# Weight words of the gated block not held back, norms and gated products at other places of the order, one root on GpSimd

## The chip, the cores and the metric

The kernel runs on one core of a Trainium2 chip. Time is device time in microseconds (us) of one execution; the engines are TensorE (PE, the matrix products), VectorE (DVE), ScalarE (ACT), GpSimd (POOL) and SyncE (SP, whose queue issues the DMA transfers). Each engine runs its own instructions in order, and semaphores make one wait for another.

## The reference

Three steps on 4 batches of 576 rows. Attention with 8 heads of 64: a local part (a band of 3 rows to each side) plus a part that is computed on rows averaged by four and repeated. Its output x (576 x 512 per batch) goes through a mixing block and a gated block; all weights and inputs are fp32.

```python
# mixing block
X = np.fft.fft(x, axis=1); X = np.fft.fft(X, axis=2)
mixed = np.real(X)
u = x + mixed
un = (u - mean(u)) / np.sqrt(var(u) + 1e-06)
ch = np.maximum(un @ w_ch1, 0.0) @ w_ch2        # 512 -> 2048 -> 512
x = u + ch
# gated block
gate = 1 / (1 + np.exp(-conv5(x, conv_w)))       # causal, per column, 5 taps
out = (gate * (x @ w_val)) @ w_out
```

## The kernel before

The rows are worked on transposed, 512 columns on 4 x 128 partitions, in 12 units of 192 rows: unit n is rows 192j to 192j+191 of batch b, n = 3b + j, counted from 0. For a unit the kernel does, one after the other: the norm (`ln`), the products with w_ch1 (`mlp_steps`: ph, L1143) and w_ch2 (pc, L1163), and the gated block (`moe2_steps`): taps, products with w_val (val, L1255), and the out tiles with w_out (L1271). Products run as three passes of f16 halves: hh and hl are the high and low half of a hidden group, uh and ul of a normed unit, yy of x, gh and gl of the gated product. Attention of a batch (scores dS, exponentials dP, their transposes dPT and dO, then sc, eT and po of the averaged part) and its Fourier products (ab, pp, pn) are spread between the units of the batch before; batch 1's stand between units 0 to 2.

The norm of a unit (`ln`, L1004 to 1071) is a chain: sum over columns (two adds uc on POOL or DVE, then st on PE, L1020), subtract (uc), square (sq, ACT), the sum again (st), variance plus epsilon (vv), an inverse square root (`root`, L1046: an integer guess and two steps; seven operations with two fused on DVE, nine on GpSimd), the multiply of uc, and the halves uh (ACT) and ul (DVE). The first ph of the unit reads them.

The weights arrive as fp32 and are cut to their words by `to_f32` (L301): one TENSOR_SCALAR (L304) and two SCALAR_TENSOR_TENSOR (L166) on DVE for each raw tile of 128 x 512. For w_val and w_out (`word_w`, L329) there are eight raws. They go through two buffers, tags "k" and "v" of one pool; the next load into a buffer can be issued once the last raw in it has been read for the last time. Afterwards the scale is measured (cv on PE, L408) and the words are converted (L380 on ACT, L166 on DVE). `to_f32` takes a gate, an instruction behind which the words are issued; for w_val and w_out it is unit 3's multiply of uc, set in `ln`.

The order is written as positions: every step is put at a number, all are sorted by it (1.0 is the length of one unit's two products; n to n+1 is unit n), and a scheduler then fixes each engine's order by readiness and by priority offsets (`U`: norms 3000, taps, outs and words 0, values 1000). S_W3 is the stretch of numbers of the weight steps, P_T that of taps, values and outs of units 0 to 2, P_LN the place of a unit's norm behind the start of the unit before it, ROOT_G the norms whose root is on GpSimd. SP's queue is in order as well.

Of the kernel before, what the change touches and what calls it, by code (L numbers as in the profile page):

```python
# [12 lines left out]
I32 = mybir.dt.int32  # L13
# [8 lines left out]
UT = 192  # L22
# [34 lines left out]
S_C1 = (0.48, 0.5)  # L57
S_N0 = -7.5
S_W2 = (-7.4, -6.9)
S_W3 = (2.0, 2.28)  # L60
N_WARM = (8, 5, 14, 2, 2, 2)
S_G1 = (-6.8, -6.7)
S_G2 = (0.2, 0.44)
P_D = {1: (0.02, 1.2), 2: (2.31, 3.3), 3: (4.4, 6.0)}
P_E = {1: (1.21, 1.75), 2: (3.35, 4.4), 3: (6.1, 7.4)}
P_L = {1: 1.9, 2: 4.8, 3: 8.5}
P_T = {0: ((2.3, 2.5), (2.6, 2.8), (3.0, 3.01)), 1: ((2.8, 3.1), (3.15, 3.35), (3.4, 3.6)), 2: ((3.4, 3.6), (3.65, 3.85), (3.9, 4.2))}
EN_G = (1,)
SUM_V = ()
LN_PE = ((0, 0), (0, 1))  # L70
S_N1 = 0.1
S_N2 = 0.9
# [3 lines left out]
P_VAL = (0.38, 0.65)  # L76
P_OUT = (1.12, 1.75)
P_LN = 0.1
ROOT_G = ((0, 1),)
S_R0 = 0.8  # L80
D1_H = 0
LN_H = ()
# [46 lines left out]
def attn_moe_kernel(ctx, tc, q_t, k_t, v_t, w1, w2, w_val, conv_t, w_out, c_feat, c_seq, c_band, c_eye, out):  # L129
    nc = tc.nc  # L130
    P = 128
# [21 lines left out]
    V, A, G, T = nc.vector, nc.scalar, nc.gpsimd, nc.tensor  # L153
# [14 lines left out]
    def mul(eng, out, a, b):  # L168
        return eng.tensor_tensor(out=out, in0=a, in1=b, op=ALU.mult)
# [4 lines left out]
    def urgent(f, key):  # L174
        if U[key]:
            with tc.high_priority(offset=U[key]):
                f()
        else:
            f()
# [91 lines left out]
    W = [wp.tile([P, 1024], F32, name="W0")]  # L271
# [16 lines left out]
    def rows(dst, src, c, c0, n):  # L288
        load(out=dst, in_=src[c * 128:(c + 1) * 128, 2 * c0:2 * (c0 + n)])
# [3 lines left out]
    def behind(gate, f):  # L293

        if gate is None:
            f()
        else:
            with tc.issue_after(gate):
                f()

    def to_f32(dst, raw, gate=lambda: None):  # L301

        r = raw.rearrange("p (n t) -> p n t", t=2)
        behind(gate(), lambda: V.tensor_scalar(out=dst, in0=r[:, :, 1], scalar1=3, scalar2=0x3FFFFFF8,  # L304
                                               op0=ALU.logical_shift_left, op1=ALU.bitwise_and))
        behind(gate(), lambda: stt(V, dst, r[:, :, 1], -0x40000000, dst, ALU.bitwise_and, ALU.bitwise_or))
        last = []
        behind(gate(), lambda: last.append(stt(V, dst, r[:, :, 0], 29, dst, ALU.logical_shift_right, ALU.bitwise_or)))
        return last[0]
# [19 lines left out]
    def word_w(i):  # L329
        if i < 16:  # L330
            raw = raws.pop(i)
            n = 1024 // len(raw)
            pos = AT[i] if i < 8 else 8
            for z, x in enumerate(raw):
                last = to_f32(W[AT[i] + 1].bitcast(I32)[:, z * n:(z + 1) * n], x,
                       lambda g=gates if pos < 4 else gates1 if pos < 8 else gates2: g.pop(0) if len(g) > 1 else g[0])
            if i == 11:
                st[0]["worded"] = last
            return
        assert "scored" in st[1]  # L340
        for a in range(2):
            raw = qkv.tile([P, 1024], I32, tag="kv"[a], name="raw")
            rows(raw, w_val if i < 18 else w_out, (i % 2) * 2 + a, 0, 512)
            to_f32(W[i + 1].bitcast(I32)[:, a * 512:(a + 1) * 512], raw, lambda: un["gate"])

    diag = W[NPOS - 1][:, 0:5 * P].rearrange("p (t c) -> p t c", t=5)
    gram = {}
# [646 lines left out]
    un = {}  # L994
# [9 lines left out]
    def ln(b, j):  # L1004
# [19 lines left out]
        uc = mainp["g"].tile([P, 4, UT], F32, tag="gh", name="u32") if head else l_t("uc", [P, 4, UT])  # L1024
        ps = colsum(uc, x)
        i = V.tensor_tensor(out=uc, in0=x, in1=ps.unsqueeze(1).to_broadcast([P, 4, UT]), op=ALU.subtract)  # L1026
# [5 lines left out]
        i = A.activation(out=sq, in_=uc, func=AF.Square)  # L1032
# [4 lines left out]
        vv = tiny.tile([P, UT], F32, tag="r2", name="vv", bufs=2) if not head else keep.tile([P, UT], F32, name="vv0")  # L1037
        e = G if (b, j) in ROOT_G else V
        if e is G or head:
# [4 lines left out]
        r1 = tiny.tile([P, UT], F32, tag="r1", name="r1", bufs=2)  # L1044
# [16 lines left out]
            return  # L1061
        root()
        r1 = r0
        i = mul(V, uc, uc, r1.unsqueeze(1).to_broadcast([P, 4, UT]))
        if (b, j) == (1, 0):
            un["gate"] = i.ins
        uh = mainp["un"].tile([P, 4, UT], F16, tag="uh", name="uh")
        ul = mainp["un"].tile([P, 4, UT], F16, tag="ul", name="ul")
        A.activation(out=uh, in_=uc, func=AF.Copy)  # L1069
# [295 lines left out]
    def put(pos, f):  # L1365
        events.append((pos, len(events), f))
# [31 lines left out]
    assert S_N0 <= S_W2[0] and 4 / 17 < S_C0[0] and 8 / 17 < S_C1[0] and S_C1[1] <= 9 / 17  # L1398
    assert S_S0[1] <= S_END <= S_F0[0] and 1 <= S_W3[0]
    put(S_END, close)  # L1400
# [11 lines left out]
    w3 = weights3_steps()  # L1412
    spread([(1.0, f) for f in w3], *S_W3)
    for n, (b, j) in enumerate(units):
        main = mlp_steps(b, j)
        spread([(1.0, f) for f in main], n, n + 1)
        if j + 1 < UPB:
            put((n + P_LN if n > 1 else S_N2) if n else S_N1, lambda b=b, j=j: urgent(lambda: ln(b, j + 1), "N"))
        ps = [P_TAP, P_VAL, P_OUT]
        if n in P_T:  # L1420
            ps = [tuple(x - n - 1 for x in p) for p in P_T[n]]
        if n == B * UPB - 2:
            ps[1:] = [tuple(1 + x for x in P_TAIL[1]), tuple(1 + x for x in P_TAIL[2])]
        if n == B * UPB - 1:
            ps[0] = P_TAIL[0]
        for g, p in zip(moe2_steps(b, j), ps):
            spread(g, n + 1 + p[0], n + 1 + p[1])
# [52 lines left out]
```

## Time and profile before

| | us |
|---|---|
| three runs | 746.18, 747.73, 747.88 |
| median | 747.73 |
| profiled execution | 745.68 |
| its span, first to last instruction | 743.9 |
| PE busy in the span | 690.7 |
| DVE, ACT, POOL busy | 473.7, 327.2, 109.8 |
| mean granted clock of PE | 0.951 |

A row of a timeline has the start of an instruction in us from the start of the span, its length, its engine and line, output and inputs by the program's names, their shapes, and in brackets how long the engine stood idle before it and which instruction ended that. Matmuls of 192 columns overlap, so their lengths add up to more than the time. In the page's slices one slice is 18.6 us; a digit is a tenth of the slice, or a tenth of full clock.

### The profile page before, as it was taken

What the parts mean: (1) busy time and instruction counts of PE and PEld (TensorE: products, weight loads), DVE (VectorE), ACT (ScalarE), POOL (GpSimd) and SP (SyncE); (2) the same over time, 40 slices, a digit from 0 to 9 for tenths busy, and PEclk for the clock granted to TensorE, in tenths of its full rate; (3) what the DMA queues carried; (4) which work ended last, traced back from release to release, by engine and by line L of the source; (5) the groups of instructions that cost most, each with busy time, mean ns of one, the idle gap of its engine ahead of it and who ended that gap; (6) DMA issues with size and microseconds to landing.
All of it is one profiled execution on the core that took longest, in us unless ns stands there. A gap on an engine that the chain in (4) does not pass through costs nothing.

```text
span 743.9 us, 18323 instructions
## 1 busy us (share of the span) xinstructions
PE 690.7 (93%) x7785; PEld 601.6 (81%) x7785; DVE 473.7 (64%) x983; ACT 327.2 (44%) x998; POOL 109.8 (15%) x158
## 2 busy tenths in 40 slices
PE   8588799999999699689988999999999999999997
PEld 4355598899899498577877879888989989999895
DVE  4988699888476777356499554846845473642424
ACT  1673364795432128745444365654422132221213
POOL 0400011511111000350030223402010010000000
PEclk9658999999999799869999999999999999999999
DMA  9965262430032160130231001001200000000001
GB/s 240 385 226 162 76 226 85 111 107 2 30 100 63 61 182 3 57 94 15 79 111 65 2 24 40 32 2 54 59 15 16 2 1 30 3 15 2 29 2 44
DMA packets 27574, 53.01 MB, mean 71 GB/s; under 512 B 2112, under 2 KB 16320, under 8 KB 26468
## 3 DMA queue, kind: packets, MB, share of 16 engines
q1 hardware_dynamic: 27492, 51.84, 21.8%
q8 instruction: 61, 1.00, 0.5%
q14 instruction: 21, 0.17, 0.1%
HBM read 45.34 MB, written 8.26 MB: 72 GB/s over the span
## 4 chain that ended last, share of the span: by engine, by line
PE 68%; DVE 19%; ACT 5%; DMA 5%; issue 1%; POOL 1%; SPq 1%; DVEq 0%; ACTq 0%; POOLq 0%
PE pc L1163 20%; PE ph L1143 20%; DVE W L166 7%; PE out L1271 6%; PE val L1255 5%; ACT dP L573 2%; PE po L780 2%; PE sc L729 2%; PE pc L1118 2%; PE dO L614 2%; DVE W L304 1%; PE ab L893 1%; PE st L1020 1%; PE dPT L594 1%; DMA raw<-in_moe_w_out_dram 1%
## 5 line engine op out<-in xcount | busy, mean ns | idle before, releaser
L1143 PE MATMUL ph<-uh,W 128*128 128x192 f16 x1408 | 200.7, 250 | 9.0 <-ACT uh L1069 9.0
L1143 PEld LDWEIGHTS <-W 128*128 128x128 f16 x2112 | 179.6, 99 | 20.8 <-issue 18.0
L1143 PE MATMUL ph<-ul,W 128*128 128x192 f16 x704 | 175.9, 250 | 2.6 <-DVE ul L1070 2.6
L1163 PE MATMUL pc<-hh,W 128*128 128x192 f16 x1232 | 171.8, 246 | 0.0
L1163 PEld LDWEIGHTS <-W 128*128 128x128 f16 x1848 | 153.3, 98 | 6.0 <-issue 4.5
L1163 PE MATMUL pc<-hl,W 128*128 128x192 f16 x616 | 150.6, 246 | 0.0
L166 DVE SCALAR_TENSOR_TENSOR hl<-ph,hh 128x384 f16<-128x384 f32 x88 | 48.4, 551 | 75.5 <-ACT hh L1147 74.9
L1147 ACT ACTIVATE hh<-ph 128x384 f16<-128x384 f32 x88 | 43.2, 490 | 121.1 <-PE ph L1143 118.1
L166 DVE SCALAR_TENSOR_TENSOR W<-X,cw,W 128x192 f32<-128x192 f32 x160 | 61.0, 437 | 0.2
L1255 PE MATMUL val<-yy,W 128*128 128x192 f16 x576 | 53.4, 247 | 1.5 <-DVE yy L166 1.5
L1255 PEld LDWEIGHTS <-W 128*128 128x128 f16 x576 | 48.5, 98 | 3.9 <-issue 2.0
L573 ACT ACTIVATE dP<-dS,dmx 128x64 f32<-128x64 f32 x160 | 47.9, 331 | 2.1 <-PE dPT L594 1.7
L1271 PE MATMUL out<-W,gh 128*128 128x512 f16 x144 | 45.9, 379 | 0.0
L573 ACT ACTIVATION_READ_ACCUMULATOR dP<-dS,dmx 128x1 f32 x160 | 36.0, 225 | 0.0
L166 DVE SCALAR_TENSOR_TENSOR X<-pc,iv,X 128x384 f32<-128x384 f32 x22 | 12.9, 613 | 24.7 <-PE pc L1163 24.7
L166 DVE SCALAR_TENSOR_TENSOR W<-W,W 128x1024 int32<-128x1024 int32 x24 | 28.3, 1214 | 0.1
L1271 PE MATMUL out<-W,gl 128*128 128x512 f16 x72 | 27.3, 379 | 0.0
L1218 ACT ACTIVATE W<-X,cw 128x192 f32<-128x192 f32 x40 | 15.6, 445 | 23.4 <-DVE X L166 18.5
L1105 PE MATMUL ph<-u,W 128*128 128x192 f32 x128 | 24.3, 345 | 1.0 <-DVE u L1026 1.0
L744 ACT ACTIVATE E<-sc,nm 72x144 f32<-72x144 f32 x64 | 23.6, 378 | 3.8 <-PE po L780 1.7
L1271 PEld LDWEIGHTS <-gh 128*128 128x128 f16 x144 | 14.1, 98 | 13.5 <-issue 0.2
L1163 PE MATMUL pc<-hh,Wz 128*128 128x192 f16 x176 | 24.8, 246 | 0.0
(246 smaller groups left out, 1224.1 us busy)
## 6 DMA issues: line engine op xcount, KB each, us to landing
W<-in_moe_w_ch_dram SPq DMA_DIRECT2D x12, 1024.0 KB
v<-in_v_dram SPq DMA_DIRECT2D x32, 144.0 KB
out_dram<-osb SPq DMA_DIRECT2D x17, 256.0 KB
vw<-in_v_dram SPq DMA_DIRECT2D x16, 256.0 KB
X<-in_q_dram SPq DMA_DIRECT2D x6, 576.0 KB
kT<-in_k_dram SPq DMA_DIRECT2D x4, 582.0 KB
X<-in_moe_w_ch_dram SPq DMA_DIRECT2D x2, 1024.0 KB
raw<-in_moe_w_ch_dram SPq DMA_DIRECT2D x4, 512.0 KB
```

What stands on the lines that cost most here:

```text
L166: return eng.scalar_tensor_tensor(out=out, in0=in0, scalar=scalar, in1=in1, op0=op0, op1=op1)
L573: A.activation(out=s_[:, z, a], in_=pss[par][:, z, a], func=AF.Exp, scale=SCALE, bias=mx[:, par, z, a:a + 1], accum_out=su[:, par, z, a:a ...
L614: d["dO"] = T.matmul(out=pos[x][par * 64:par * 64 + 64, a2, o:o + nq], lhsT=vw[g][row, 2 * z + hf, c:c + D], rhs=pts[z][row, par, a2, hf * ...
L729: T.matmul(out=pss[par][:, qc], lhsT=d["qkT"][r, 0, a, qc * QC:(qc + 1) * QC], rhs=d["qkT"][r, 1, a, :], start=True, stop=True,)
L744: A.activation(out=E[:, qc], in_=ps[:, qc], func=AF.Exp, scale=SCALE / 16, bias=nm[:, qc:qc + 1], accum_out=su[:, qc:qc + 1],)
L1105: i = T.matmul(out=ps[:, e], lhsT=W[AT[kc * 2 + m // 8] + 1][:, o:o + 128], rhs=u()[:, kc, :], start=(kc == 0), stop=(kc == 3))
L1143: T.matmul(out=ps[:, e], lhsT=w1_ap(pw, kc, 2 * g + e), rhs=uh[px][:, kc, :], start=(t == 0), stop=(t == 11))
L1147: A.activation(out=h_, in_=ps, func=AF.Relu)
L1163: T.matmul(out=ps[m // 2][:, m % 2], lhsT=w2_ap(pw, kk, m), rhs=x[px][:, e, :], start=(kk == 0 and (pw, px) == (0, 0) and m % 2 == 0), sto ...
L1218: A.activation(out=m, in_=x, func=AF.Copy, scale=w)
L1255: T.matmul(out=ps[:, e], lhsT=wv_ap(pw, kc, 2 * mh + e), rhs=m_["y"][px][:, kc, :], start=(t == 0), stop=(t == 11))
L1271: T.matmul(out=ps, lhsT=(gh, gl)[px][:, kc, t * 128:(t + 1) * 128], rhs=wo_ap(pw, kc), start=(n == 0), stop=(n == 11))
```

## The change

There are five edits. The words of w_val and w_out lose their gate, and their stretch of positions moves from 2.0 to 2.28 to 1.91 to 2.0. Taps, values and outs of units 0, 1 and 2 move up, by about 0.3 to 0.5. Norms of units 4 and 5 (put while units 3 and 4 run) move from n + 0.1 to n - 0.15. Unit 3's root moves from DVE to GpSimd, and with it its vv from DVE to ACT. Line numbers of the changed kernel are one higher than before up to L1064 and one lower behind it.

```diff
-S_W3 = (2.0, 2.28)
+S_W3 = (1.91, 2.0)
...
-P_T = {0: ((2.3, 2.5), (2.6, 2.8), (3.0, 3.01)), 1: ((2.8, 3.1), (3.15, 3.35), (3.4, 3.6)), 2: ((3.4, 3.6), (3.65, 3.85), (3.9, 4.2))}
+P_T = {0: ((2.0, 2.1), (2.12, 2.3), (2.5, 2.51)), 1: ((2.35, 2.6), (2.65, 2.85), (2.9, 3.1)), 2: ((2.95, 3.2), (3.25, 3.45), (3.5, 3.8))}
...
-ROOT_G = ((0, 1),)
+P_LNS = {3: -0.15, 4: -0.15}
+ROOT_G = ((0, 1), (1, 0))
...
-            to_f32(W[i + 1].bitcast(I32)[:, a * 512:(a + 1) * 512], raw, lambda: un["gate"])
+            to_f32(W[i + 1].bitcast(I32)[:, a * 512:(a + 1) * 512], raw)
...
-        i = mul(V, uc, uc, r1.unsqueeze(1).to_broadcast([P, 4, UT]))
-        if (b, j) == (1, 0):
-            un["gate"] = i.ins
+        mul(V, uc, uc, r1.unsqueeze(1).to_broadcast([P, 4, UT]))
...
-            put((n + P_LN if n > 1 else S_N2) if n else S_N1, lambda b=b, j=j: urgent(lambda: ln(b, j + 1), "N"))
+            put((n + P_LNS.get(n, P_LN) if n > 1 else S_N2) if n else S_N1, lambda b=b, j=j: urgent(lambda: ln(b, j + 1), "N"))
```

In the order's rows a number behind a name tells one tile from another of that name; the numbers of one tile differ between the two kernels.

PE before, at the last sums of unit 4's norm (uc_3685 and sq_3691) and the products of attention ahead of the unit's first ph:

```order
L614 MATMUL dO_3649<-PT_3647,vw_2996 64x58 x2
L614 MATMUL dO_3650<-PT_3647,vw_2996 64x58 x2
L1020 MATMUL st_3688<-uc_3685,ones_105 128x192
L1020 MATMUL st_3695<-sq_3691,ones_105 128x192
L594 MATMUL dPT_3742<-eye_102,dP1_3466 128x128 x2
L594 MATMUL dPT_3742<-eye_102,dP1_3475 128x128 x2
L594 MATMUL dPT_3749<-eye_102,dP1_3466 128x128 x2
L594 MATMUL dPT_3749<-eye_102,dP1_3475 128x128 x2
L614 MATMUL dO_3756<-PT_3747,vw_2999 64x58 x8
```

PE now, at the last sum of the same norm (sq_3618); uh_2680 and ul_2681 are unit 3's, gh_2952 and gl_2953 unit 0's:

```order
L1142 LDWEIGHTS W1_114
L1142 MATMUL ph_3992<-uh_2680,W1_114 128x192
L1142 LDWEIGHTS W1_114
L1142 MATMUL ph_3992<-ul_2681,W1_114 128x192
L1021 MATMUL st_3622<-sq_3618,ones_105 128x192
L1270 LDWEIGHTS gh_2952
L1270 MATMUL out_3664<-W17_122,gh_2952 128x512
L1270 LDWEIGHTS gl_2953
L1270 MATMUL out_3664<-W17_122,gl_2953 128x512
L1270 LDWEIGHTS gh_2952
L1270 MATMUL out_3664<-W17_122,gh_2952 128x512
L1270 LDWEIGHTS gh_2952
```

The sum stood next to the last products ahead of unit 4's first ph; now it stands inside unit 3's products, ahead of unit 0's out tiles. Between it and unit 4's first ph there are now 293 matmuls with 192 columns, and others.

DVE before, in unit 2's norm and behind it (hl_2481 is a low half of unit 1):

```order
L169 TENSOR_TENSOR uc_1811<-uc_1811,r0_1825 128x768
L1070 TENSOR_TENSOR ul_1836<-uc_1811,uh_1835 128x768
L172 TENSOR_TENSOR X_125<-X_125,base_1169 128x576
L166 SCALAR_TENSOR_TENSOR hl_2481<-ph_2454,hh_2479 128x384
L263 TENSOR_REDUCE f2_v1_2001<-tot_1999 128x1
L265 TENSOR_SCALAR f2s_v1_2003<-f2_v1_2001 128x1
L247 TENSOR_SCALAR p2a_2007<-f2s_v1_2003 128x1
L166 SCALAR_TENSOR_TENSOR bq1_4593<-f2s_v1_2003,ff_1576 128x1
```

DVE now, at the same place; raw_2709 and raw_2719 are the third and fourth raw of the "k" buffer:

```order
L305 TENSOR_SCALAR W19_123<-raw_2709 128x512
L170 TENSOR_TENSOR r1_1826<-r0_1825 128x192
L167 SCALAR_TENSOR_TENSOR W19_123<-raw_2709,W19_123 128x512
L167 SCALAR_TENSOR_TENSOR r1_1826<-r1_1826,vv_1823 128x192
L167 SCALAR_TENSOR_TENSOR W19_123<-raw_2709,W19_123 128x512
L167 SCALAR_TENSOR_TENSOR r0_1825<-r1_1826,r0_1825 128x192
L170 TENSOR_TENSOR uc_1811<-uc_1811,r0_1825 128x768
L1069 TENSOR_TENSOR ul_1836<-uc_1811,uh_1835 128x768
L305 TENSOR_SCALAR W19_123<-raw_2719 128x512
L173 TENSOR_TENSOR X_125<-X_125,base_1169 128x576
L167 SCALAR_TENSOR_TENSOR W19_123<-raw_2719,W19_123 128x512
L167 SCALAR_TENSOR_TENSOR hl_2481<-ph_2454,hh_2479 128x384
```

The words of w_val and w_out, which stood behind unit 3's multiply of uc some 70 rows later, now stand one raw at a time inside this norm and between the hl splits around it; four of the eight raws stand ahead of hl_2481 or directly beside it, the others up to the Fourier splits FL of batch 1.

ACT before, up to unit 3's uh (uh_2678) and the squares of w_val behind it:

```order
L1147 ACTIVATE hh_3283<-ph_3258 128x384
L1147 ACTIVATE hh_3394<-ph_3369 128x384
L1032 ACTIVATE sq_2660<-uc_2654 128x768
L1069 ACTIVATE uh_2678<-uc_2654 128x768
L407 ACTIVATE sqv_2841<-W17_122 128x512
L407 ACTIVATE sqv_2844<-W17_122 128x512
```

ACT now, from the conversion of w_val to unit 3's uh (uh_2680):

```order
L381 ACTIVATE W15_121<-W17_122,s_wv_2746 128x1024 x2
L1196 ACTIVATE yy_2920<-X_132,s_y0_2806 128x768
L1041 ACTIVATE vv_2666<-st_2664 128x192
L381 ACTIVATE W17_122<-W19_123,s_wo_2785 128x1024 x2
L566 ACTIVATE dmx_3134<-dmx_3134 128x8
L574 ACTIVATE dP1_3139,dsu_3135<-dS_3114,dmx_3134 128x64 x4
L574 ACTIVATE dP1_3144,dsu_3135<-dS_3116,dmx_3134 128x64 x4
L1358 ACTIVATE W19_123<-eye_102,cw_108 128x128 x5
L1217 ACTIVATE W19_123<-X_132,cw_108 128x192 x4
L1261 ACTIVATE gh_2952<-tap_2843 128x2x192
L1068 ACTIVATE uh_2680<-uc_2654 128x768
L1261 ACTIVATE gh_2952<-tap_2843 128x2x192
```

Unit 3's uh stood directly behind its square; now vv, the conversions of both weights, the first half of yy, the exponentials dP, the diagonals and the taps of a unit stand ahead of it.

## Rows read from the trace of the kernel before

**Rows 1.** The page: busy time of the engines; granted clock in 40 slices.
```profile
PE 690.7 (93%) x7785; PEld 601.6 (81%) x7785; DVE 473.7 (64%) x983; ACT 327.2 (44%) x998; POOL 109.8 (15%) x158
...
PEclk9658999999999799869999999999999999999999
```

**Rows 2.** Windows: busy us (instructions) of each engine; PE clock, DMA share, GB/s.
```profile
163.00:187.00 24.00, 24.00 (x312) 22.04 (x310) 20.72 (x49) 15.19 (x41) 3.53 (x4) 1.00 0.03 11
187.00:210.00 23.00, 23.00 (x257) 20.44 (x256) 13.46 (x31) 8.82 (x26) 5.21 (x5) 1.00 0.15 52
...
244.00:258.00 14.00, 6.70 (x36) 5.01 (x34) 10.61 (x21) 2.56 (x4) 1.58 (x2) 0.64 0.23 73
...
309.00:330.00 21.00, 13.37 (x158) 11.45 (x157) 9.06 (x16) 9.01 (x25) 12.33 (x15) 0.51 0.22 61
...
385.00:410.00 25.00, 20.33 (x214) 17.54 (x212) 24.93 (x57) 8.49 (x19) 2.71 (x9) 0.93 0.27 83
410.00:744.00 334.00, 327.53 (x3802) 295.95 (x3799) 173.78 (x386) 120.32 (x327) 37.68 (x50) 1.00 0.06 21
```

**Rows 3.** Timeline of PE: start, us, operation [idle before <-releaser].
```profile
250.56 0.48 PE L1143 MATMUL ph<-uh,W 128*128 128x192 f16 x2 [5.91 <-ACT uh L1069]
252.43 0.32 PE L1143 MATMUL ph<-ul,W 128*128 128x192 f16 x1 [1.39 <-DVE ul L1070]
...
308.60 0.71 PE L729 MATMUL sc<-qkT 64*72 64x144 f32 x4 [1.80 <-ACT dP L573]
...
311.68 1.01 PE L1020 MATMUL st<-uc,ones 128*128 128x192 f32 x2 [0.48 <-ACT X L620]
316.42 1.01 PE L1020 MATMUL st<-sq,ones 128*128 128x192 f32 x2 [3.73 <-POOL sq L172]
...
324.57 0.48 PE L1143 MATMUL ph<-uh,W 128*128 128x192 f16 x2 [2.74 <-ACT uh L1069]
325.74 0.32 PE L1143 MATMUL ph<-ul,W 128*128 128x192 f16 x1 [0.69 <-DVE ul L1070]
```

**Rows 4.** Timeline of DVE: unit 3's root, a raw, unit 4's root.
```profile
245.28 0.63 DVE L1047 TENSOR_SCALAR r<-vv 128x192 int32<-128x192 int32 x1
...
248.28 0.36 DVE L166 SCALAR_TENSOR_TENSOR r<-r,r 128x192 f32<-128x192 f32 x1
...
256.66 0.43 DVE L304 TENSOR_SCALAR W<-raw 128x512 int32<-128x512 int32 x1 [3.08 <-DMA raw<-in_moe_w_val_dram]
...
317.86 0.77 DVE L1047 TENSOR_SCALAR r<-vv 128x192 int32<-128x192 int32 x1
```

**Rows 5.** Timeline of GpSimd: unit 1's root, first and last; beside unit 4's root.
```profile
108.50 0.35 POOL L1047 TENSOR_SCALAR r<-vv 128x192 int32<-128x192 int32 x1 [1.95 <-ACT vv L1040]
...
114.65 0.59 POOL L169 TENSOR_TENSOR r<-r,r 128x192 f32<-128x192 f32 x1
...
317.51 1.00 POOL L172 TENSOR_TENSOR uc<-X 128x384 f32<-128x384 f32 x1 [1.14 <-PE st L1020]
```

**Rows 6.** Timeline of ACT: conversions of w_val, first taps.
```profile
269.07 2.19 ACT L380 ACTIVATE W<-W,s_wv 128x1024 f16<-128x1024 f32 x2 [1.69 <-DVE s_wv L251]
...
283.63 1.48 ACT L1218 ACTIVATE W<-X,cw 128x192 f32<-128x192 f32 x4
```

**Rows 7.** Operations on raw: ns minimum/median/maximum, first and last start.
```profile
L166 DVE SCALAR_TENSOR_TENSOR W<-raw,W x24: 672/681/693, 95.0 to 274.1; 128x512 int32<-128x512 int32 x24
L304 DVE TENSOR_SCALAR W<-raw x12: 417/426/830, 92.1 to 270.7; 128x512 int32<-128x512 int32 x12
```

**Rows 8.** Timeline of DVE in the stretch 187 to 210: its two longest stops.
```profile
200.70 1.14 DVE L166 SCALAR_TENSOR_TENSOR X<-pc,iv,X 128x384 f32<-128x384 f32 x2 [2.60 <-PE pc L1163]
204.35 0.56 DVE L166 SCALAR_TENSOR_TENSOR hl<-ph,hh 128x384 f16<-128x384 f32 x1 [2.51 <-ACT hh L1147]
```

**Rows 9.** Timeline of SyncE's queue: issue of two raws of w_val.
```profile
253.01 1.81 SPq L190 DMA_DIRECT2D raw<-in_moe_w_val_dram  x2
```

## The prediction, made before the changed kernel was run

> **What bounds the kernel now.** The page comes first: TensorE (PE) is busy for 690.7 of 743.9 us, and the row of granted clocks holds full speed in most slices and falls to 6 or 7 tenths around the middle [rows 1]. So PE's order is the bound, and time can be won only where PE stands or runs at the lower of its two levels (1.2 in place of 2.4 GHz). The windows tell where that is [rows 2]: from 410 us on PE is busy 327.53 of 334.00 us at clock 1.00, in 163 to 210 it never stops, and the losses lie at 244 to 258 (6.70 busy of 14, clock 0.64), 309 to 330 (13.37 of 21, clock 0.51) and 385 to 410 (20.33 of 25, clock 0.93). PE's own rows name the first two: they are the starts of units 3 and 4, where the last sum of a norm (st, L1020) is followed at once by the first product that reads the normed rows (ph, L1143) [rows 3].
>
> Unit 3's start: PE waits 5.91 us for uh, then 1.39 us for ul [rows 3], together 7.3. The windows give 6.70 us of work, about 0.7 of it before the stop; a mean clock of 0.64 over 14 us means some 10 us at half speed, 4 of them idle, so 6 us of work lose 3.0. Sum: 10.3 us lost. Unit 4's start: 1.80 (sc behind dP), 0.48 and 3.73 (st behind sq), 2.74 (ph behind uh) and 0.69 (ul) are 9.4 us idle [rows 3]; the clock of 0.51 puts 20.5 of the 21 us at half speed, and of these 7.6 are idle, so 12.9 us of work lose 6.4. Sum: 15.9 us, the dearest place of the program after its start.
>
> **The change part by part.** *Norms up.* For unit 4 the order of the change has st over uc and sq ahead of the out tiles of unit 0, with 293 matmuls of 192 columns and some other work between the last st and unit 4's first ph; before there were only the last transposes and dO products between them. From 410 us on 327.53 us of busy PE hold 3802 matmuls of all kinds, 0.086 us each [rows 2], so the 293 alone are 25 us. The chain from the end of the last st to the first ph was 317.43 to 324.57, 7.1 us [rows 3]. It fits under 25 us more than three times. So all 15.9 us can go: also the lower clock, since what came ahead of it was PE's idle time. It goes to nothing if another wait stands in the same place: sc behind dP (1.80) is not touched by this, so I keep 1 to 2 us of it in the range. Term: -15.9, from -16 to -10 (the idle time left half in place). The same shift for unit 5 touches the stretch 385 to 410, which has 4.67 us idle and a clock of 0.93; waits of the next batch's mixing and of val products share it, and the change doesn't move these. I take nothing, from -4 to +4.
>
> *Root of unit 3 on GpSimd, and work put between.* Before, the norm is short: DVE's seven operations run from 245.28 to 248.64, 3.4 us, and uc, uh and ul follow [rows 4]. The nine on GpSimd are in the trace at unit 1: 108.50 to 115.24, 6.74 us [rows 5], so the chain grows by 3.3 us. It grows further by queues: on ScalarE (ACT) vv now stands behind the conversion of w_val's words and yy, and uh behind eight dP exponentials, the diagonals, four first taps and a gh. Rows price these: 2.19 us for two conversions, 1.48 for four taps [rows 6]; in all some 10 us of ACT work, most of which has its inputs early. On DVE the multiply of uc stands behind four conversions, yy and two adds, at 1 us each at the most. Against that stands cover on PE that wasn't there: 25 matmuls of unit 2's end, two dS groups and the 48 val matmuls of unit 0, then a further dS group. At 0.086 us each the 73 f16 matmuls are 6.3 us, and the dS groups (over 60 small products) about as much again. Before, the cover was nil and the wait 7.3. Now a chain of about 7.3 + 3.3 + 6 (queues) = 17 us meets 12 us of cover: 5 us idle, and in proportion some 1.5 us for the clock. Term: 6.5 in place of 10.3, so -3.8, from -9 (cover holds everything) to +6 (the queues add up to 15 us).
>
> *Words not gated.* This is the term on the other side. A raw costs DVE one operation of 0.43 us and two of 0.68 [rows 7], 1.79 us; the eight raws of w_val and w_out are 14.3 us. They ran in 249 to 275, where DVE was waiting for PE or DMA anyway (3.08 us idle for one raw [rows 4]); taking them away there frees nothing that PE waits for beyond unit 3's start. In the new order they stand one by one between the hl splits of units 1 and 2: by the order, four raws fall in the stretch 163 to 187 and four in 187 to 210. In the first DVE has 24.00 - 20.72 = 3.28 us free, in the second 23.00 - 13.46 = 9.54 [rows 2]. PE is full in both, so what overflows delays PE. First stretch: 4 x 1.79 = 7.2 less 3.28 is 3.9 us. Second: 7.2 fits by volume, and its idle pieces, 2.60 and 2.51 us, lie ahead of X and of an hl [rows 8]. But a raw must also land: the eight go through two buffers, so its load is issued only behind the last word of the raw before it. Issue to first word was 3.65 us before (253.01 to 256.66 [rows 4, 9]). Where the new order has 2 to 3 us of DVE work between (the third raw, behind the second; the last two of the second stretch), DVE stands for 1 to 2 us and holds the next hl; three such places make about 2.6 us beyond what is idle anyway. PE's short stops there cost perhaps 2 us more at the lower clock, an estimate in proportion to unit 3's start, where 7.3 us idle brought 3.0. Term: 3.9 + 2.6 + 2 = +8.5; the ends are +1.5 (all volume: 14.3 less 12.8) and +14 (double waits).
>
> *Values, outs and taps up.* The work is the same; it is spent ahead of and after unit 3's start as cover, counted above. ACT and DVE become denser there: 73 matmuls need tap products, gl and gh sooner. I add +2 for small waits, 0 to 4.
>
> **The sum.** -15.9 - 3.8 + 8.5 + 2 = -9.2. On the profiled execution of 745.68 us (span 743.9 and 1.8 around it) that gives 736.5. The profile lies 2.05 us under the median of 747.73, so in terms of the median: 738.5. A measurement of this kernel can tell about 0.3% (2.2 us) from no change.
>
> **The rivals.** *Words free, 731.5.* If DVE absorbs the words and only the overflow by volume of 1.5 us is left, the sum is -16.2. For it: 9.54 us idle in the second stretch [rows 2], and hl in the first stretch could slip where PE has other work. Against it: PE has no idle time there and the first stretch overflows. *Root on GpSimd, 748.6.* Then unit 3's start becomes 16.6 us in place of 6.5: 10.3, plus 3.3 for the longer root, plus 3 for the operations of DVE that run beside it. The row for this: DVE's root operations took 0.77 us at 317.86 with GpSimd busy beside them, and 0.36 us at 248.28 without [rows 4, 5]. The sum is then +0.9, no change. The Trainium skill says of this in "SBUF — State Buffer", section "SBUF: two separate sides", that VectorE and GpSimd lock a shared port pair for a whole instruction and the loser stands; the doubling in the rows agrees. Its "GPSIMD Engine Reference", section "Engine selection", advises VectorE for elementwise work on a tile, GpSimd being about half as fast with two inputs, and 6.74 beside 3.4 us agrees. By these two rules the sum would be +0.9; by the rows of the queues alone, where both roots end under cover, it is the forecast's -9.2.
>
> *The words hold DVE, slower, 753.4.* Every raw but the first two waits for its whole load: 6 x 3.65 = 21.9 us, plus 14.3 of words, less 12.8 idle, is 23.4 on the path in place of 8.5, and the sum is -15.9 - 3.8 + 23.4 + 2 = +5.7. It decides against the change as soon as the words cost over 17.7 us. For it: DVE runs in order, so a word whose raw hasn't landed stops every hl, root and lsu behind it, and SP's queue, in order as well, has the dx, dr and kT transfers of the next batch behind the raws. Against it: in most places 3 us or more of other DVE work stands between two raws of one buffer. That the change doesn't do what it says, since a queue on GpSimd or ACT holds sq of unit 4 until its ph is due, would leave half of the 15.9 in place; the sum would be about -1, and this case goes with the second rival.
>
> **How the numbers follow.** Chances: forecast 0.52, words free 0.17, no change 0.15, words hold DVE 0.16. So faster by over 0.3% 0.69, within 0.3% 0.15, slower by over 0.3% 0.16. The range leaves out a tenth at each side: the low end takes in the words-free case with a further 3.7 us at unit 3's start, 728.0; the high end takes in the no-change case and some of the slower one, 751.0.
>
> **What would show it.** In the profile after: the ph of unit 4 follows other matmuls without a stop, and the half-clock slices in the middle shrink from two places to one. At unit 3's start an idle time of 3 to 7 us ahead of ph or out, its releaser uh, gh or yy. In 163 to 210, PE's busy time falls under the stretch's length, with stops behind hl, eT or po of 1 to 3 us each, and DVE shows stops behind raw. If PE stays full there, the words were free; if it stops for over 15 us there, or if unit 4's st still stands directly ahead of its ph, the prediction is wrong.

## The result, and the profile after

The changed kernel takes 727.99 us (median of 4 runs, 726.95 to 728.06), against 747.13 (median of 4) before: a ratio of 0.9741, with a 95% interval of 0.9724 to 0.9758, or 19.1 us less. The prediction was 738.5 with a range from 728.0: the sign is right, the gain is twice what was forecast, and the time lies a hair under the range.

The profiled execution of the changed kernel has a span of 726.3 us, 17.6 less than before. The page, as in [rows 1], with PE's own slices added; a slice is now 18.2 us:

```profile
span 726.3 us, 18324 instructions
...
PE 678.0 (93%) x7785; PEld 590.3 (81%) x7785; DVE 463.3 (64%) x975; ACT 326.1 (45%) x999; POOL 120.4 (17%) x167
...
PE   7578898899989969999999999999999999999997
...
PEclk9758999999999989999999999999999999999999
```

The dips of the clock around the middle, 7, 8 and 6 tenths before, are one 8. PE is busy 678.0 us in place of 690.7, for the same matmuls: at half clock they are longer. Windows of the changed kernel, columns as in [rows 2]:

```profile
163.00:223.00 60.00, 56.04 (x665) 50.22 (x664) 53.09 (x112) 27.46 (x75) 11.39 (x11) 1.00 0.32 100
244.00:275.00 31.00, 24.52 (x285) 18.75 (x285) 26.91 (x64) 18.50 (x58) 12.21 (x14) 0.89 0.03 11
275.00:340.00 65.00, 63.82 (x818) 53.41 (x816) 35.36 (x99) 41.88 (x144) 16.51 (x21) 1.00 0.25 72
340.00:410.00 70.00, 67.34 (x825) 60.52 (x824) 53.43 (x112) 31.38 (x101) 11.78 (x18) 1.00 0.16 51
410.00:726.00 316.00, 310.29 (x3588) 282.83 (x3585) 156.61 (x359) 109.56 (x281) 32.77 (x42) 1.00 0.06 21
```

The same stretches of the kernel before:

```profile
163.00:223.00 60.00, 59.63 (x735) 54.72 (x733) 42.42 (x93) 28.42 (x77) 10.82 (x14) 1.00 0.14 44
244.00:275.00 31.00, 23.47 (x214) 19.67 (x212) 24.83 (x48) 7.37 (x11) 1.58 (x2) 0.83 0.41 129
275.00:340.00 65.00, 54.66 (x757) 47.47 (x755) 38.29 (x96) 40.80 (x150) 18.38 (x22) 0.84 0.19 52
340.00:410.00 70.00, 65.33 (x680) 55.72 (x679) 52.12 (x127) 32.84 (x91) 7.04 (x12) 0.98 0.22 72
```

The first stretch got worse: PE's free time in 163 to 223 grew from 0.37 to 3.96 us, while DVE's busy time grew from 42.42 to 53.09. The second holds unit 3's start in both kernels, with the clock at 0.89 for 0.83. The third, with unit 4's start, lost its stops: 1.18 us free at clock 1.00 in place of 10.34 at 0.84. The fourth has 2.66 us free for 4.67.

What answers [rows 3] is this. Unit 4's first ph has no stop ahead of it any more, in any row. At unit 3's start val of unit 0 comes first now, and PE stops inside it:

```profile
257.83 0.74 PE L1254 MATMUL val<-yy,W 128*128 128x192 f16 x7 [2.03 <-DVE yy L167]
```

and then three times around the first ph:

```profile
264.14 0.39 PE L1270 MATMUL out<-W,gh 128*128 128x512 f16 x1 [0.88 <-ACT gh L1261]
265.94 0.32 PE L1142 MATMUL ph<-uh,W 128*128 128x192 f16 x2 [1.40 <-ACT uh L1068]
268.42 0.61 PE L1270 MATMUL out<-W,gl 128*128 128x512 f16 x1 [2.17 <-DVE gl L167]
```

A sum over PE's stops (each with the row that ends it) and over the stretches at half clock, before against after, in us of time lost:

| place | before | after | difference | predicted |
|---|---|---|---|---|
| 163 to 223, stages of units 1 and 2 | 0.4 | 3.8 | +3.5 | +8.5 |
| unit 3's start | 10.3 | 9.1 | -1.2 | -3.8 |
| unit 4's start, with sc ahead of it | 15.9 | 0 | -15.9 | -15.9 |
| 340 to 410 (before: stops 4.7, clock 1.7, all behind 385) | 6.4 | 2.7 | -3.7 | 0 |
| small stops elsewhere behind 270 us | 3.6 | 2.4 | -1.2 | +2 |
| the start of the program, to 145 us | | | +0.8 | 0 |
| sum | | | -17.7 | -9.2 |

The span fell by 17.6. The start of the program varies by more than that row from execution to execution: the first stop at a Fourier product behind FH comes at 213.76 us before, at 215.84 us with only unit 3's root moved and at 217.83 us with only two sums of unit 4 moved, edits of work that comes later. A difference of 1 or 2 us between two single traces is read with that in mind.

### The profile page after: what moved, and what is told of

Same layout as the page of the kernel before. It is cut to its first block, busy times and chain, and to the rows that moved or that the text cites. A ratio compares the mean times of both kernels' runs of the same rounds, so it can differ in the third digit from the quotient of the medians.

```text
span 726.3 us, 18324 instructions
## 1 busy us (share of the span) xinstructions
PE 678.0 (93%) x7785; PEld 590.3 (81%) x7785; DVE 463.3 (64%) x975; ACT 326.1 (45%) x999; POOL 120.4 (17%) x167
## 4 chain that ended last, share of the span: by engine, by line
PE 59%; DVE 23%; DMA 7%; ACT 6%; POOL 2%; issue 1%; SPq 1%; ACTq 0%; DVEq 0%; POOLq 0%
PE pc L1162 18%; PE ph L1142 17%; DVE W L167 10%; PE out L1270 6%; PE val L1254 4%; DMA raw<-in_moe_w_out_dram 2%; DMA v<-in_v_dram 2%; ACT dP L574 2%; DVE W L305 2%; PE ab L894 1%; PE po L781 1%; PE dO L615 1%; DVE X L173 1%; DVE qkT L626 1%; DMA X<-in_moe_w_ch_dram 1%
## 5 line engine op out<-in xcount | busy, mean ns | idle before, releaser
L1142 PE MATMUL ph<-uh,W 128*128 128x192 f16 x1408 | 196.9, 247 | 1.4 <-ACT uh L1068 1.4
L1142 PEld LDWEIGHTS <-W 128*128 128x128 f16 x2112 | 176.4, 98 | 10.3 <-issue 7.6
L1142 PE MATMUL ph<-ul,W 128*128 128x192 f16 x704 | 173.8, 247 | 0.0
L1162 PEld LDWEIGHTS <-Wz 128*128 128x128 f16 x264 | 22.1, 98 | 5.4 <-issue 2.9
L1117 PE MATMUL pc<-h,W 128*128 128x192 f32 x128 | 23.0, 330 | 1.8 <-DVE tr L170 1.2
```

The costliest lines, as they stand in the source:

```text
L1117: T.matmul(out=c["ps"][m // 2][:, m % 2], lhsT=W[9 + g][:, o:o + 128], rhs=hs[g // 2][:, g % 2, e, :], start=(kk == 0 and m % 2 == 0), sto ...
L1142: T.matmul(out=ps[:, e], lhsT=w1_ap(pw, kc, 2 * g + e), rhs=uh[px][:, kc, :], start=(t == 0), stop=(t == 11))
L1162: T.matmul(out=ps[m // 2][:, m % 2], lhsT=w2_ap(pw, kk, m), rhs=x[px][:, e, :], start=(kk == 0 and (pw, px) == (0, 0) and m % 2 == 0), sto ...
```

## Experiments

Two theories stood at first. B is the prediction's: the norms' shift of 0.25 frees unit 4's start, and the words are a cost. A: what pays is that the words no longer wait for unit 3's norm. In the code cuts `...` stands for lines left out. All times below are medians, before at 746.9 to 747.4 in the same comparisons.

**The gate put back.** The changed kernel with

```diff
-            to_f32(W[i + 1].bitcast(I32)[:, a * 512:(a + 1) * 512], raw)
+            to_f32(W[i + 1].bitcast(I32)[:, a * 512:(a + 1) * 512], raw, lambda: un["gate"])
...
-        mul(V, uc, uc, r1.unsqueeze(1).to_broadcast([P, 4, UT]))
+        i = mul(V, uc, uc, r1.unsqueeze(1).to_broadcast([P, 4, UT]))
+        if (b, j) == (1, 0):
+            un["gate"] = i.ins
```

> The changed kernel with the gate back on the words of w_val and w_out (behind unit 3's multiply of uc); all else as changed. Theory A (what pays is that the words no longer stand behind unit 3's norm; only then does unit 4's norm come ahead of its first product by much): the order has 1 matmul of 192 columns between unit 4's last st and its first ph, as in the kernel before, so the 15.9 us lost at that start come back, and with them most of 385 to 410; 742 to 750 us. Theory B, that of the prediction (the norms' shift by 0.25 frees unit 4's start, and the words without a gate are a cost of some 8 us): 718 to 724 us.

Measured: 750.28 us (745.32 to 755.46), ratio 1.004 (1.0012 to 1.0068), a hair above theory A's range. The whole gain goes, although norms, root and taps are as changed. It doesn't go where theory A said: of the 15.9 us only some 5 come back at unit 4's start (300 to 340 us), while 340 to 412 us, with 6.4 us lost before, loses 20.

**The words alone.** The kernel before with

```diff
-S_W3 = (2.0, 2.28)
+S_W3 = (1.91, 2.0)
...
-            to_f32(W[i + 1].bitcast(I32)[:, a * 512:(a + 1) * 512], raw, lambda: un["gate"])
+            to_f32(W[i + 1].bitcast(I32)[:, a * 512:(a + 1) * 512], raw)
...
```

> The kernel before with the words alone freed (no gate, their stretch at 1.91 to 2.0). Theory A: the order alone puts 230 matmuls between unit 4's last st and its first ph, against 1 before, so most of the gain comes from this edit: 728 to 736 us. Theory B: the words cost 8.5 us and nothing pays for it: 752 to 758 us.

Measured: 732.5 us, ratio 0.9802 (0.9783 to 0.982). This one edit brings 14.6 of the 19.1 us.

**The norms put back**, and **the norms alone**: the changed kernel with the first pair of lines; the kernel before with `P_LNS = {3: -0.15, 4: -0.15}` and the second pair.

```diff
-P_LNS = {3: -0.15, 4: -0.15}
+P_LNS = {}
...
-            put((n + P_LN if n > 1 else S_N2) if n else S_N1, ...
+            put((n + P_LNS.get(n, P_LN) if n > 1 else S_N2) if n else S_N1, ...
```

> The changed kernel with the norms of units 4 and 5 at n + 0.1 again. Theory A: unit 4's norm is still 161 matmuls (14 us) ahead of its first product, more than the 7 us of its chain, so 727 to 731 us. Theory B: the 15.9 us of unit 4's start come back, 740 to 746 us.

> The kernel before with only the norms of units 4 and 5 at n - 0.15. Theory A: the order still has 1 matmul between unit 4's last st and its first ph; 743 to 749 us. Theory B of the prediction: 15.9 us less, 729 to 735 us.

Measured: 730.8 us with the norms back (ratio 0.9785, 0.976 to 0.981), and 745.84 with the norms alone (0.9984, 0.9961 to 1.0008). So the shift is worth nothing clear of noise by itself and some 3 us beside the freed words; theory B falls on all four runs. The norms alone do something at unit 4's start: in that trace PE loses 7.1 us at 300 to 340 us in place of 15.8. But 376 to 412 us then loses 10.4 in place of 6.4, and the time stays. Whatever makes PE stand there can be moved along the program without being removed.

**The root put back**, and **the root alone**:

```diff
-ROOT_G = ((0, 1), (1, 0))
+ROOT_G = ((0, 1),)
```

> The changed kernel with unit 3's root on DVE. Seen in the changed kernel's trace: the nine operations on GpSimd took 8.5 us and the multiply of uc waited 1.64 us for them. If the root's length sets unit 3's start, DVE's 3.4 us give 1 to 3 us back: 725 to 727 us. If DVE is the tighter engine there (it converts both weights in the same stretch), the seven operations stand in its queue ahead of yy or behind the conversions and the start grows: 729 to 733 us.

> The kernel before with only unit 3's root on GpSimd. In that kernel uh stands behind the root alone, and the cover is 1 matmul. By the rows, 6.7 to 8.5 us in place of 3.4 lengthen unit 3's stop by 3.3 to 5.1 us: 749 to 752 us. If something else stands there anyway: 745 to 748 us.

Measured: 732.07 us without it (0.9798, 0.9775 to 0.9821), 4.1 us slower than the changed kernel; and 750.19 with it alone (1.004, 1.0014 to 1.0066), 2.8 us slower than before. The same edit has both signs, and the traces show why. In the kernel with the root alone, unit 3's first ph stands longer, 8.76 us where [rows 3] has 5.91:

```profile
255.50 0.48 PE L1143 MATMUL ph<-uh,W 128*128 128x192 f16 x2 [8.76 <-ACT uh L1069]
```

In the changed kernel with the root on DVE, its seven operations stand one by one between the conversions of both weights and the taps. From the first to the last they take 15.7 us (256.04 to 271.76), where [rows 4] has 3.4 and GpSimd takes 8.5 in the changed kernel:

```profile
256.04 0.64 DVE L1048 TENSOR_SCALAR r<-vv 128x192 int32<-128x192 int32 x1
...
271.41 0.35 DVE L167 SCALAR_TENSOR_TENSOR r<-r,r 128x192 f32<-128x192 f32 x1
```

**Taps, values and outs put back:**

```diff
-P_T = {0: ((2.0, 2.1), (2.12, 2.3), (2.5, 2.51)), 1: ((2.35, 2.6), (2.65, 2.85), (2.9, 3.1)), 2: ((2.95, 3.2), (3.25, 3.45), (3.5, 3.8))}
+P_T = {0: ((2.3, 2.5), (2.6, 2.8), (3.0, 3.01)), 1: ((2.8, 3.1), (3.15, 3.35), (3.4, 3.6)), 2: ((3.4, 3.6), (3.65, 3.85), (3.9, 4.2))}
```

> The changed kernel with taps, values and outs of units 0 to 2 at their old numbers. If the moved val products are what covers unit 3's start, that start loses some 4 us more (its cover before the first ph is smaller) and the time is 730 to 733 us; if the words' early end is enough (values come as soon as their weights stand), 727 to 729 us.

Measured: 728.09 us, ratio 0.9733 (0.9708 to 0.9758), the changed kernel's own time. The edit does nothing that can be measured. With old taps and the root on DVE as well:

> The changed kernel with the taps at their old numbers and unit 3's root on DVE: words and norms moved alone. With the root on DVE the changed kernel took 732.1 us, with old taps 728.1. If the two edits are independent, 732 us; if the root on GpSimd pays only because the values stand close to unit 3's start, 728 us.

Measured: 729.51 us, ratio 0.9753 (0.9723 to 0.9784). That lies between the two expectations, and the intervals are too wide to choose: by the medians the root on GpSimd is worth 1.4 us with old taps, against 4.1 with new ones. In the profiled executions with old taps (728.5 and 731.96 us) PE's stops between 255 and 280 us come to 5.0 us with the root on GpSimd and to 8.8 with it on DVE. So it isn't shown that its worth hangs on the new taps.

**What the words cost DVE.** The words are put together by three operations from the two halves of a 64-bit number, as which the weights lie in memory (the text ahead of the prediction calls them fp32 there). The changed kernel without the second and third of them for w_val and w_out, so that these weights lack sign and low bits:

```diff
+        if one:
+            return
         behind(gate(), lambda: stt(V, dst, r[:, :, 1], -0x40000000, dst, ALU.bitwise_and, ALU.bitwise_or))
```

> The changed kernel with one of the three DVE operations for each raw of w_val and w_out (the other two, which add the sign and the low bits, are left out, so the gated block works with other weights): 16 operations of 0.68 us, 10.9 us of DVE, are gone, the loads and their waits stay. In the changed kernel PE stands for 3.84 us in 163 to 223 us behind hl, FL and FH. If that is DVE's volume, it falls to under 1.5 us and the time to 724 to 726 us; if it is the wait for the loads of the raws, 3 us or more of it stay and the time is 727 to 729 us.

Measured: 723.55 us (719.96 to 728.59), ratio 0.9671 (0.9609 to 0.9734). The runs spread over 8.6 us and the interval overlaps the changed kernel's, so the time decides nothing; the traces do. These are PE's stops of the changed kernel in 160 to 226 us:

```profile
177.90 0.24 PE L1162 MATMUL pc<-hl,W 128*128 128x192 f16 x1 [0.86 <-DVE hl L167]
...
208.84 0.24 PE L1162 MATMUL pc<-hl,Wz 128*128 128x192 f16 x1 [0.79 <-DVE hl L167]
...
215.42 0.32 PE L894 MATMUL ab<-feat,FL 128*97 128x129 f16 x2 [0.49 <-DVE FL L167]
...
217.96 0.32 PE L894 MATMUL ab<-feat,FL 128*97 128x129 f16 x2 [1.09 <-DVE FL L167]
...
221.61 0.43 PE L894 MATMUL ab<-feat,FH 128*97 128x128 f16 x4 [0.61 <-ACT FH L872]
```

Without the two operations all of them but the last are gone, while 3.83 us of DVE's waits for raws remain. A stop of another kind appears, on GpSimd's product for E, so the sum in this stretch, 3.6 us, doesn't fall under the 1.5 us that were expected:

```profile
166.96 0.44 PE L773 MATMUL eT<-eye,E 72*72 72x72 f32 x4 [2.95 <-POOL E L170]
```

So the 3.2 us behind hl and FL hang on the two operations and not on the landing of the raws by itself. They are not plain volume, though. In the changed kernel DVE waits for raws five times, together 4.95 us: 0.58, 0.54, 0.69 and the two below. And the word operation directly ahead of the late hl (208.25) and of the second late FL (217.10) takes 1.58 and 1.90 us, where most take 0.68:

```profile
206.28 0.43 DVE L305 TENSOR_SCALAR W<-raw 128x512 int32<-128x512 int32 x1 [1.61 <-DMA raw<-in_moe_w_out_dram]
206.74 1.58 DVE L167 SCALAR_TENSOR_TENSOR W<-raw,W 128x512 int32<-128x512 int32 x1
...
213.46 0.43 DVE L305 TENSOR_SCALAR W<-raw 128x512 int32<-128x512 int32 x1 [1.53 <-DMA raw<-in_moe_w_out_dram]
...
215.27 1.90 DVE L167 SCALAR_TENSOR_TENSOR W<-raw,W 128x512 int32<-128x512 int32 x1
```

GpSimd is at work beside both:

```profile
206.37 1.40 POOL L173 TENSOR_TENSOR X<-X,base 128x576 f32<-128x576 f32 x1 [4.35 <-ACT base L785]
214.80 1.83 POOL L858 TENSOR_TENSOR fs<-X 128x577 f32<-128x577 f32 x1 [7.03 <-DVE fF L866]
```

The 0.90 and 1.22 us by which these two are longer are about as much as the stops that follow (0.79 and 1.09). How much of the 3.2 us is volume, how much the raws and how much GpSimd beside DVE, no run separates.

**What the gate held.** Still open was why words that end 55 us earlier free a norm two units later. PE's results land in PSUM. The two pools that matter here, tags s and t, have two banks each and give them out by turns: a tile that is asked for later waits until an earlier one of its tag is done. Two turns looked guilty. Tag t: cv and tot of the two weights' scales stand ahead of batch 2's first dS. Tag s: val of unit 0 stands ahead of batch 2's dPT, dO, eT and po, and of unit 4's st. In the kernel before, dS comes 0.2 us behind tot:

```profile
277.43 0.31 PE L257 MATMUL tot<-ss_wo,ones 128*128 128x1 f32 x2
277.60 0.27 PE L541 MATMUL dS<-bandb 128*128 128x256 bf16 x1
```

First unit 4's st alone was taken out of the turn of tag s:

```diff
-LN_H = ()
+LN_H = ((1, 1),)
```

> The kernel before, words gated as before; only the two st sums of unit 4's norm go to the PSUM pool of the ph tiles (tag h) in place of the pool of two banks (tag s) that dPT, dO, eT, po, st, val and out take turns in. Theory A1 (the gate held unit 4's st by the turns: val of unit 0, late because its weights' words were late, was given its bank before st, so st had to wait): 320 matmuls stand between its last st and its first ph, the stop of unit 4 goes, and the time is 729 to 737 us with no word moved. Theory A2 (the gate held st because DVE, ACT and GpSimd had their hands full with words and conversions at 250 to 285): the norm stays late on those engines, and the time is 743 to 748 us.

Measured: 744.7 us, ratio 0.9971 (0.9938 to 1.0004). A miss for A1, and instructive: unit 4's stop is gone (between 299 and 375 us PE's stops come to 1.0 us), but the time comes back elsewhere, about half of it at 376 to 408 us (9.8 us of stops for 4.7, and more work at the lower clock), in stops behind batch 2's Fourier steps and others. The time lies in A2's range, but not for its reason, since unit 4's norm no longer holds PE:

```profile
380.13 0.39 PE L1271 MATMUL out<-W,gl 128*128 128x512 f16 x1 [1.74 <-DVE gl L166]
...
383.93 0.67 PE L893 MATMUL ab<-feat,FH 128*97 128x128 f16 x4 [1.89 <-ACT FH L871]
...
388.33 1.92 PE L1255 MATMUL val<-yy,W 128*128 128x192 f16 x11 [1.70 <-DVE yy L166]
```

Then the sums of the scales were moved to tag s, alone and with that st:

```diff
-        ps = pst("cv", [P, 512])
+        ps = pst("cvw", [P, 512])
...
-            gram[key] = pst("cv", [P, P]) if key == "wo" else ...
+            gram[key] = pst("cvw", [P, P]) if key == "wo" else ...
...
-        ps = pst("tot", [P, n])
+        ps = pst("totw" if name == "wo" else "tot", [P, n])
```

> The kernel before, words gated as before; the sums over w_val and w_out (cv and tot of the scales) are put into the PSUM pool with tag s, so that batch 2's first score tiles (dS, tag t) need not wait for their turn behind them. Theory C (what the gate held was batch 2's attention: its dS could start only when the last word of w_out, at 274 us, was summed; everything up to the norm of unit 6 came some 15 to 20 us late, and PE ran out of other work at unit 4's start and at 385 to 410): dS starts before unit 3 in the order, the first fs of batch 2 comes at 350 to 360 in place of 372 us, and the time is 730 to 738 us. Theory D (the volume of words and conversions on DVE and ACT between 250 and 285 us is what made it late): fs stays at 368 to 373 us and the time at 743 to 748 us.

> As the run with the sums of the weights in tag s, and with unit 4's st in the pool of the ph tiles as well. Theory C: both turns in PSUM that the gated words held are undone, and the gain is that of the changed kernel without its price in 163 to 223 us (3.5 us) but with unit 3's start as before: 724 to 733 us. Theory D: 741 to 748 us.

Measured: 743.49 us (0.9948, 0.9925 to 0.9971) and 741.92 (0.9928, 0.9908 to 0.9949). By their times, and by fs, both fall in theory D's ranges. The first turn is undone, and little follows: dS is 40 us earlier, but the first dPT still comes right behind the last val of unit 0 (PE's rows of the run with the sums alone):

```profile
237.24 0.27 PE L542 MATMUL dS<-bandb 128*128 128x256 bf16 x1
...
290.32 1.07 PE L1256 MATMUL val<-yy,W 128*128 128x192 f16 x11
...
293.12 0.60 PE L595 MATMUL dPT<-eye,dP 128*128 128x128 f32 x4
```

Batch 2's first Fourier step, fs on DVE, moves only from 371.88

```profile
371.88 0.76 DVE L857 TENSOR_TENSOR fs<-X 128x577 f32<-128x577 f32 x1 [0.34 <-ACT X L810]
```

to 369.68 us:

```profile
369.68 0.76 DVE L858 TENSOR_TENSOR fs<-X 128x577 f32<-128x577 f32 x1 [0.34 <-ACT X L811]
```

A second turn could still be in the way. So dPT and dO of batch 2 were taken out of the turn of tag s too, with words, conversions and val as late as before:

```diff
+HB = (2,)
...
-                ps = pst("dPT", [P, 2, 2, P])
+                ps = ps_h.tile([P, 2, 2, P], F32, tag="h", name="dPT") if b in HB else pst("dPT", [P, 2, 2, P])
...
-                pos = [... if first else pst("dO", [P, 2, nt]) for x in range(2)]
+                pos = [... if first else ps_h.tile([P, 2, nt], F32, tag="h", name="dO") if b in HB else pst("dO", [P, 2, nt]) for x in range(2)]
```

> The kernel before, words gated; sums over w_val and w_out in tag s, and st of unit 4 and dPT and dO of batch 2 in the pool of the ph tiles (tag h), so none of them has to wait for its turn behind val of unit 0. Theory C (turns): the first dPT of batch 2 comes well before val of unit 0, before 270 us in place of 292, the last scores of the averaged part (354 us before) come under 340, fs under 360; the time falls below 740 us unless PE stands behind vw, whose loads also wait for the raws in the two buffers (270 us). Theory D (volume): dPT comes early too but the exponentials and lowres steps stay late, fs at 368 us or later and 743 us or more.

Measured: 738.19 us, ratio 0.9874 (0.9843 to 0.9905). PE's rows: dPT is now 40 us ahead of val, and val as late as in the other gated kernels (282.9 us before, 286.6 with the sums alone):

```profile
247.50 0.66 PE L596 MATMUL dPT<-eye,dP 128*128 128x128 f32 x4
...
287.50 0.48 PE L1257 MATMUL val<-yy,W 128*128 128x192 f16 x2 [3.09 <-ACT yy L1199]
```

fs comes at 353 us, 18 us earlier, about as in the changed kernel (357.17):

```profile
353.48 0.76 DVE L859 TENSOR_TENSOR fs<-X 128x577 f32<-128x577 f32 x1 [0.35 <-ACT X L812]
```

The last scores sc of batch 2's averaged part come at 337.6 us, 18 us earlier as well. The windows of this run,

```profile
244.00:310.00 66.00, 50.60 (x590) 37.55 (x588) 53.79 (x112) 36.78 (x126) 19.12 (x22) 0.82 0.33 99
310.00:410.00 100.00, 98.98 (x1150) 87.00 (x1148) 72.88 (x167) 48.77 (x150) 14.42 (x22) 1.00 0.19 59
```

beside those of the kernel before,

```profile
244.00:310.00 66.00, 55.76 (x730) 48.26 (x729) 46.67 (x107) 33.59 (x124) 6.97 (x8) 0.92 0.27 80
310.00:410.00 100.00, 87.69 (x927) 74.60 (x922) 68.58 (x162) 47.43 (x128) 20.04 (x29) 0.88 0.24 71
```

show that from 310 to 410 us PE's free time falls from 12.3 to 1.0 us, at full clock. The words and conversions are as many and as late as before here, so for what PE lost behind 310 us theory D falls: it was the turns that batch 2's attention had to take behind val. It isn't the whole gain. This run is 8.8 us under the kernel before and 10.2 above the changed one, and in 244 to 310 it is worse than before: 15.4 us free for 10.2, at clock 0.82 for 0.92, with the longest stops behind yy (3.09 us) and gl (2.97). There attention, words and conversions now come at one time; that the late words are the price is likely but not shown. That both turns have to go is shown for one order only: the first alone gave 3.9 us, with unit 4's st 5.5, with dPT and dO as well 8.8. The second alone was not run.

**The same sums in the changed kernel:** with the words free, the turn of tag t could still have cost something there.

> The changed kernel with the sums over w_val and w_out in tag s. There dS comes directly behind these sums at 252 us. If batch 2's attention still sets stops after that, its earlier start gives 1 to 5 us: 723 to 727 us. If it no longer does, the new order of sums and st in tag s costs at unit 3's start: 728 to 732 us.

Measured: 731.69 us (730.68 to 738.48), ratio 0.981 (0.974 to 0.9881). It is in the second range and 3.7 us above the changed kernel by the medians, though the intervals overlap; undoing the turn of tag t no longer gains anything there.

**Unit 4's adds on DVE,** with old taps:

```diff
-LN_V = ((0, 0), (0, 2), (1, 0), (2, 0), (3, 0))
+LN_V = ((0, 0), (0, 2), (1, 0), (1, 1), (2, 0), (3, 0))
```

> The changed kernel with taps, values and outs at their old numbers and the adds of unit 4's norm on DVE in place of GpSimd. In the changed kernel these adds stand on GpSimd at 252.9 to 255.4 us, directly ahead of unit 3's root, which starts 0.6 us behind its vv. If they delay unit 3's root and slow DVE's conversions beside them (2.12 us in place of 1.28), 1 to 2 us go: 725 to 727 us. If the adds on DVE stand in the way of the conversions, 728 to 731 us.

Measured: 726.12 us (725.87 to 730.32), in the first range, ratio 0.9724 (0.9688 to 0.976). It is the lowest median of a kernel that computes all, 1.9 us under the changed kernel, but the intervals overlap; it isn't shown to be faster.

## Why the prediction was right and wrong

The forecast was 9.2 us of gain and the sum of the table is 17.7. Of the 8.5 between them, the words were priced 5.0 too high, 340 to 410 brought 3.7 that were taken at 0, small waits 3.2; unit 3's start fell short by 2.6 and the start of the program by 0.8.

**The step that failed** is this one, of the words: "taking them away there frees nothing that PE waits for beyond unit 3's start". The reason given was that DVE was waiting anyway in 249 to 275 us; it was busy for 24.83 of the 31 us from 244 to 275. The words alone brought 14.6 us. What they held was val of unit 0, and behind val, by the turns in PSUM, batch 2's attention. So the edit that the prediction put down as a cost is the one that pays.

**Norms up, -15.9.** The size is right to the tenth, the cause is wrong, and the match is luck: 15.9 is all that was lost at that place. The reading "the order of the change has st ahead of the out tiles" is true, but it was put down to the edit that names these norms. With the norms alone, unit 4's last st still has 1 matmul of 192 columns between it and the first ph, with the words alone 230, with all five edits 293; and the norms alone took 745.84 us. Each edit's own order was there to be read, and the prediction read only that of all five together.

**385 to 410, taken at 0.** It was -3.7 (340 to 410 in the table). The waits there were said not to be moved by the change. They are: batch 2's attention runs ahead of its Fourier steps, and its dPT stood behind val, whose weights stood behind the gate. fs moved from 371.88 to

```profile
357.17 1.49 DVE L858 TENSOR_TENSOR fs<-X 128x577 f32<-128x577 f32 x1 [0.34 <-ACT X L811]
```

**Words not gated, +8.5.** It measured +3.5 in the table, between the rival's +1.5 and the forecast. Four of the five PE stops are behind DVE, as said, but of 0.5 to 1.1 us each where 1 to 3 were named, and two of them are behind FL. Mis-sized were two terms. The overflow of the first stretch was put at 3.9 and PE lost 0.9 there: DVE's work ran later without PE standing for it. And the clock, +2, was 0: in 163 to 223 it stayed at 1.00. Behind the start of the program it fell at unit 3's start alone, behind stops of 2.03, 0.88 and 1.40 us. The term of 2.6 for later waits was near, with 3.0, but for another reason in part: word operations that are longer beside GpSimd were not in it.

**Unit 3's start, -3.8.** It was -1.2. The forecast of 5 us idle became 6.5: 2.03 in val, 0.88, 1.40 and 2.17. Two links of the chain were longer than put, both in DVE's and GpSimd's rows. The four conversions on DVE were taken at 1 us each at the most; they took 2.12, 1.55, 1.34 and 1.51. Those of w_val:

```profile
252.87 2.12 DVE L167 SCALAR_TENSOR_TENSOR W<-W,s_wv,W 128x1024 f16<-128x1024 f32 x1
...
254.97 1.55 DVE L167 SCALAR_TENSOR_TENSOR W<-W,s_wv,W 128x1024 f16<-128x1024 f32 x1
...
264.05 0.96 DVE L170 TENSOR_TENSOR uc<-uc,r 128x768 f32<-128x768 f32 x1 [1.64 <-POOL r L170]
```

and GpSimd beside them:

```profile
252.90 1.00 POOL L173 TENSOR_TENSOR uc<-X 128x384 f32<-128x384 f32 x1 [8.28 <-PE st L1021]
253.98 1.45 POOL L173 TENSOR_TENSOR uc<-uc 128x192 f32<-128x192 f32 x1
255.52 1.21 POOL L1048 TENSOR_SCALAR r<-vv 128x192 int32<-128x192 int32 x1
256.81 1.33 POOL L170 TENSOR_TENSOR r<-r 128x192 f32<-128x192 f32 x1
...
263.43 0.59 POOL L170 TENSOR_TENSOR r<-r,r 128x192 f32<-128x192 f32 x1
```

The conversion took 2.12 us while GpSimd added for unit 4; the same operation took 1.28 us at 162.93 in this trace. The root took 8.5 us (255.52 to 264.02) where [rows 5] has 6.74, and the multiply of uc waited 1.64 us for it. The rival with the longer root named this and put it at +6.3 by itself; as one edit it is +2.8 on the kernel before, and -4.1 inside the changed one, where DVE's queue stretches the root to 15.7 us. Its pair of rows compares two different operations, though: the one of 0.77 us at 317.86 took 0.63 at 245.28 [rows 4]. The doubling holds for one operation against itself: the root's r<-r,vv (L166) took 0.77 us at 319.43 and 0.36 at 246.71 of the kernel before. The Trainium skill, in "SBUF — State Buffer", section "SBUF: two separate sides", says that VectorE, in an operation with two inputs from SBUF among others, and GpSimd share a port pair, that whichever starts first holds it for the whole instruction, and that the other stands. The 2.12 us agree in direction, and so does the root's first operation on GpSimd: 1.21 us, with DVE's second conversion still running beside it (to 256.52), where [rows 5] has 0.35.

**Small waits, +2.** They were -1.2.

**The rivals.** "Words free", 731.5, was the nearest in time, yet its reason (DVE absorbs the words) is only part of it: it too gave the freed words no gain of their own. "The words hold DVE" fell: DVE waited 4.95 us for raws in all, not 21.9.

## What to carry to other kernels

Where tiles take turns in a few PSUM banks, a late producer holds every tile that is asked for after it, even of other work: look for the stage that starts within a microsecond of something it doesn't read. Where two such turns stand in a row, undoing the first shows little of what both hold (3.9 us of 8.8 here). And before a gain is given to one edit of several, read the order with that edit alone.

## What the runs showed that was not expected

DVE had 53.09 us of work in the 60 us from 163 to 223 and PE lost 3.8 us; most of the words cost PE nothing. The root on GpSimd changes its sign with what stands beside it: +2.8 us in the kernel before, -4.1 in the changed one. And a loss on PE can move: at unit 4's start it went with one PSUM turn undone or with the norms alone, and about half of it came back some 70 us later.
